# Order of half-width matmuls and of three groups of loads in the gradient tail of a memory transformer

## The chip, the core and the metric

The kernel runs on one core of a Trainium2 chip. The metric is the device time of one execution in microseconds (us), as the median of several runs. The engines named here are TensorE (PE; its weight loads are shown apart as PEld), VectorE (DVE), ScalarE (ACT), GpSimd (POOL) and SyncE (SP). POOL and SP issue most of the transfers (DMAs) of this kernel: SP those of its own queue, plain and transposing, POOL those of another.

## The reference

One transformer layer, forward and backward. Attention runs over segments of 32 rows that carry 8 memory rows from one segment to the next, and a gated feed-forward block follows. All ten results (the output and nine gradients) are returned.

```
x = A_x                                   # 1 x 2048 x 448
h = x + A(layernorm(x), mem0, Wq, Wk, Wv, Wo)     # 64 segments, one after another
h2 = h + (silu(n @ w_gate) * (n @ w_up)) @ w_down  # n = layernorm(h)
outputs: h2 and the gradients of A_x, mem0, Wq, Wk, Wv (448 x 16 x 256 each),
         Wo (16 x 256 x 448), w_gate, w_up (448 x 1792), w_down (1792 x 448)
```

In each segment `A` concatenates the memory (8 rows) and 32 rows of x, projects them to q, k and v for 16 heads of 256, applies a masked softmax, and its first 8 output rows are the memory of the next segment. So the gradients of Wq, Wk, Wv and Wo are products over 2048 token rows and 512 memory rows, which is 20 blocks of 128 rows: 16 token blocks and 4 memory blocks. The gradients of the feed-forward weights are products over the 16 token blocks.

## The kernel before

The kernel has a forward chain over 64 segments, a feed-forward phase, a backward chain over the 64 segments, and a tail (`tail_phase`, from L1289) that computes the weight gradients from operands that the earlier phases have stored in DRAM. The change concerns the tail and the first loads for it.

**Units of the tail.** First comes the gradient of Wo, in two halves of the columns. `rows_by_d` (L1392) takes 6, 5 or 5 column tiles at a time; with every one of the 20 blocks of rows it does one matmul for each tile (L1397), of an X_o tile against a block of DCt, the stored gradient of the output. Then come the halves v0, v1, k0, k1, q0, q1 of the gradients of Wv, Wk and Wq (`att`, L1420), with `up_grad` for w_gate (DGP) after v0 and for w_up (DU) after k0, and at the end w_down, again with `rows_by_d`.

**d_by_e (L1365)** computes 448 rows of a gradient by 1024 columns. The 448 rows are three full tiles of 128 and a rest of 64. For each block there are six full-width matmuls (L1375: three row tiles by two column groups of 512) and two half-width ones (L1380), which put their 64 rows into the two halves of one accumulator. Full-width ones come in groups of four blocks. The half-width ones follow each group where the argument `frees` is true; where it is false they all come at the end of the pass, after the last group. `att` and `up_grad` call `d_by_e` twice for each unit: the first pass (q = 0, or p0 = 0) with `frees` false, the second with `frees` true.

**Memory blocks.** The four memory blocks of a unit are not stored in the layout that the tail needs. `load_m` (L1336) makes three steps for each: `fetch` (L1340), a DMA from POOL into one of two buffers; `pack`, a copy half by VectorE (L1345) and half by ScalarE (L1347); and `turn`, twice eight transposes on PE (L1354) into the one transposing bank, each emptied by a copy (L75 or L76) into a ring slot. In a first pass they are put ahead of the groups of four blocks: the pack of memory block 0 and the fetch of block 2 before block 0; turn 0, pack 1 and fetch 3 before block 4; turn 1 and pack 2 before block 8; turn 2 and pack 3 before block 12; turn 3 before block 16. The transposes are recorded to issue after `k.last_mm`, the last matmul recorded then. The fetches of blocks 0 and 1 are made in the pass before.

**Order.** A scheduler orders each engine's instructions from the recorded program, so that a line of the program and its place in a queue need not be the same. VectorE, ScalarE, POOL and SP take their instructions in that order. On SP each load waits for the landing of the load eight before it, and POOL keeps a like rule.

**Loads for the tail.** `_TailLoads` (L314) hands out ring slots. In the last segment of the backward chain (s == 0) `grads(0)` loads DCt: four loads for the memory blocks (L342), then eight that gather the token blocks row by row (L346 and L347, 24 and 8 partitions each). Then `outs(0, 7, 0, 6)` loads the first six column tiles of X_o for the first seven blocks in the order of use, in which the four memory blocks come first. More calls of `outs` follow. Each load is recorded to issue after `k.last_load`, the last load of the backward chain. The gradient of w_down needs grad_out, which is loaded by POOL (L1471) into the space in which HN, the operand of `up_grad`, has lain.

Of the kernel before, what the change touches and what calls it, by code (L numbers as in the profile page):

```python
# [15 lines left out]
P = 128  # L16
# [297 lines left out]
class _TailLoads:  # L314
# [12 lines left out]
    def ring(self):  # L327
        if self.first:
            return self.first.pop(0)
        self.n += 1  # L330
        return self.slots[(self.n - 1) % len(self.slots)]

    def grads(self, part):
        k, D, S, NT, M, SEG = self.k, self.k.D, self.k.S, self.k.NT, self.k.M, self.k.SEG
        sync, DHb = k.nc.sync, k.dr["DHb"]
        dcx = DHb[0:S, 0:D].rearrange("(t r i) d -> r i t d", r=4, i=SEG)
        dcm = DHb[S:, 0:D].rearrange("(t r m) d -> r m t d", r=4, m=M)
        dc8 = DHb[0:S, 0:D].rearrange("(g s i) d -> g s i d", s=16, i=SEG)
        if part == 0:
            for g in range(k.NB - NT):  # L340
                with k.tc.issue_after(k.last_load.ins):
                    sync.dma_start(out=self.DCt[:, NT + g], in_=dc8[g, :, 0:M])  # L342
        for r in range(4):
            if part == 0:
                with k.tc.issue_after(k.last_load.ins):
                    sync.dma_start(out=self.DCt[32 * r:32 * r + 24, :NT], in_=dcx[r, M:SEG])  # L346
                    sync.dma_start(out=self.DCt[32 * r + 24:32 * r + 32, 4:NT], in_=dcm[r, :, 4:NT])  # L347
            else:
                sync.dma_start(out=self.DCt[32 * r + 24:32 * r + 32, 0:4], in_=dcm[r, :, 0:4])
# [682 lines left out]
def backward_chain(k: _K):  # L1032
    nc, tc = k.nc, k.tc
    S, D, M, H, Dh, HD = k.S, k.D, k.M, k.H, k.Dh, k.HD
    SEG, L, NSEG, NT, KC, DP, MC, DC = k.SEG, k.L, k.NSEG, k.NT, k.KC, k.DP, k.MC, k.DC
# [95 lines left out]
    for s in range(NSEG - 1, -1, -1):  # L1131
# [12 lines left out]
        with k.prio.crit():  # L1144
            pss = [k.ps1() for _ in range(4)]
            for j in range(MC):
                c = cj(j)
                b, jj = divmod(j, 8)
                for kc in range(KC):
                    with tc.issue_after(k.last_dh.ins) if s == NSEG - 1 and j == 0 and kc == 0 else nullcontext():  # L1150
                        nc.tensor.matmul(pss[b][:, jj * L:(jj + 1) * L], lhsT=WoT_sb[:, kc, c * P:(c + 1) * P],  # L1151
                                         rhs=do_roll[:, kc, sl, :], start=(kc == 0), stop=(kc == KC - 1))
# [17 lines left out]
                                         start=(dc == 0), stop=(dc == DC - 1), skip_group_check=True)  # L1170
            if s == 0:
                k.tl.grads(0)
                k.tl.outs(0, 7, 0, 6)
            pD3 = pD[:, 0:8 * L].rearrange("p (h n) -> p h n", n=L)
            prod = k.f32("f2", 8 * L, "prod")[:].rearrange("p (h n) -> p h n", n=L)
            nc.vector.scalar_tensor_tensor(out=prod, in0=pD3, scalar=k.scale, in1=P_sb, op0=ALU.mult, op1=ALU.mult)
# [30 lines left out]
            for h in range(8):  # L1207
                for g in range(2):
                    nc.tensor.matmul(pT[64 * g:64 * g + L, h * L:(h + 1) * L], lhsT=dS_bd[:, h, g, :],
                                     rhs=ident[:, 64 * g:64 * g + L], start=True, stop=True, skip_group_check=True)  # L1210
# [78 lines left out]
def tail_phase(k: _K):  # L1289
    nc, tc = k.nc, k.tc  # L1290
    S, D, M, H, Dh, HD, F = k.S, k.D, k.M, k.H, k.Dh, k.HD, k.F
    SEG, L, NSEG, NT, KC, DP, MC, DC, FC = k.SEG, k.L, k.NSEG, k.NT, k.KC, k.DP, k.MC, k.DC, k.FC
# [6 lines left out]
    NB = k.NB  # L1299
# [4 lines left out]
    HC = A(0, NB, D)  # L1304
# [5 lines left out]
    def resbuf():  # L1310
        ri[0] += 1
        return res_b[ri[0] % len(res_b)]

    def accs(n):
        return [k.ps1() for _ in range(min(n, 5))] + [k.fx1() for _ in range(max(0, n - 5))]
# [3 lines left out]
    def evac(out, in_):  # L1319
        eng = "vs"[k._evac_i % 2]  # L1320
        k._evac_i += 1
        k.last_ev[eng] = k.evac(out, in_, eng)

    def load_x(nm, hf):
        tiles = {}
        for t in (range(NT) if nm != "o" else order):
            x_t = ring()
            src = dr["X_" + nm][t][:, hf * 2048:(hf + 1) * 2048]
            if nm == "o":
                nc.sync.dma_start(out=x_t, in_=src)  # L1330
            else:
                nc.sync.dma_start_transpose(out=x_t.rearrange("p (j n) -> p j n", n=P), in_=src)
            tiles[t] = x_t
        return tiles
# [27 lines left out]
    tl.outs(0, NB, 11, 16)  # L1362
    xo = tl.x

    def d_by_e(lhs_of, rhs_of, nblk, widths, store, at=None, frees=True):  # L1365

        pa = accs(7)
        for b0 in range(0, nblk, 4):
            for fn in (at or {}).get(b0, ()):
                fn()  # L1370
            for b in range(b0, min(nblk, b0 + 4)):
                for kc in range(KC - 1):
                    for g in range(2):
                        w = widths[g]
                        k.last_mm = nc.tensor.matmul(pa[2 * kc + g][:, 0:w], lhsT=lhs_of(b)[:, kc * P:(kc + 1) * P], rhs=rhs_of(b, g),  # L1375
                                         start=(b == 0), stop=(b == nblk - 1), skip_group_check=True)
            for b in range(b0, min(nblk, b0 + 4)) if frees else range(nblk) if b0 + 4 >= nblk else ():
                for g in range(2):
                    w = widths[g]
                    k.last_mm = nc.tensor.matmul(pa[6][64 * g:64 * g + 64, 0:w], lhsT=lhs_of(b)[:, (KC - 1) * P:D], rhs=rhs_of(b, g),  # L1380
                                     start=(b == 0), stop=(b == nblk - 1), skip_group_check=True)
        for i in range(6):
            kc, g = divmod(i, 2)
            res = resbuf()
            evac(res[:, 0:widths[g]], pa[i][:, 0:widths[g]])
            store(kc, g, res[:, 0:widths[g]])
        res = resbuf()
        for g in range(2):
            evac(res[64 * g:64 * g + 64, 0:widths[g]], pa[6][64 * g:64 * g + 64, 0:widths[g]])
            store(KC - 1, g, res[64 * g:64 * g + 64, 0:widths[g]])  # L1390

    def rows_by_d(lhs_of, rhs_of, nblk, n, store):  # L1392
        pa = accs(n)
        m = len(nblk) - 4
        for bi, i in [(bi, i) for bi in range(m) for i in range(n)] + [(bi, i) for i in range(n) for bi in range(m, m + 4)]:
            b = nblk[bi]
            k.last_mm = nc.tensor.matmul(pa[i][:, 0:D], lhsT=lhs_of(b, i), rhs=rhs_of(b), start=(bi == 0), stop=(bi == m + 3))  # L1397
        for i in range(n):
            res = resbuf()
            evac(res[:, 0:D], pa[i][:, 0:D])  # L1400
            store(i, res[:, 0:D])
# [15 lines left out]
    HN = W(0, NB, D)  # L1417
    halves = [(nm, oi, hf) for (nm, oi) in (("v", 5), ("k", 4), ("q", 3)) for hf in range(2)]

    def att(hi, mem, after):  # L1420
        nm, oi, hf = halves[hi]
        o2 = OUT[oi].rearrange("d h e -> d (h e)")
        xt = load_x(nm, hf)
        for g in range(NG):
            xt[NT + g] = ring()
        for q in range(2):
            at = {}
            if q == 0:
                (f0, p0, t0), (f1, p1, t1), (f2, p2, t2), (f3, p3, t3) = mem
                at = {0: [p0, f2], 4: [lambda: t0(xt[NT]), p1, f3], 8: [lambda: t1(xt[NT + 1]), p2],  # L1430
                      12: [lambda: t2(xt[NT + 2]), p3], 16: [lambda: t3(xt[NT + 3])]}
            elif after is not None:
                at = {12: [after[0][0], after[1][0]]}

            def st(kc, g, r, q=q, hf=hf, o2=o2):
                e0 = (16 * g + 8 * hf + 4 * q) * P
                nc.gpsimd.dma_start(out=o2[kc * P:min(D, (kc + 1) * P), e0:e0 + 512], in_=r)  # L1437

            def rhs(b, g, q=q, xt=xt):
                return xt[b].rearrange("p (cl g n) -> p cl g n", g=2, n=P)[:, 4 * q:4 * q + 4, g, :]  # L1440
            d_by_e(lambda b: HC[:, b, :], rhs, NB, (512, 512), st, at, q == 1)

    def up_grad(nm, oi, after):
        xt = []
        for t in range(NT):
            x_t = ring()
            nc.sync.dma_start(out=x_t[:, 0:F], in_=dr[nm][t * P:(t + 1) * P, :])
            xt.append(x_t)
        for p0 in (0, 1024):
            ws = (512, min(512, F - p0 - 512))  # L1450

            def st(kc, g, r, p0=p0, oi=oi):
                f0 = p0 + 512 * g
                nc.gpsimd.dma_start(out=OUT[oi][kc * P:min(D, (kc + 1) * P), f0:f0 + r.shape[-1]], in_=r)

            def rhs(b, g, p0=p0, ws=ws, xt=xt):
                return xt[b][:, p0 + 512 * g:p0 + 512 * g + ws[g]]
            d_by_e(lambda b: HN[:, b, :], rhs, NT, ws, st, {8: [after[0][0], after[1][0]]} if p0 else None, p0 > 0)

    mems = [load_m(nm, hf) for (nm, _, hf) in halves] + [None]  # L1460
    mems[0][0][0]()
# [1 line left out]
    for hi in range(len(halves)):  # L1463
        att(hi, mems[hi], mems[hi + 1] if hi not in (0, 2) else None)
        if hi == 0:
            nc.gpsimd.dma_start(out=HN[:, 0:NT, :], in_=dr["HN"].rearrange("(t p) d -> p t d", p=P))
            up_grad("DGP", 7, mems[1])
        if hi == 2:
            up_grad("DU", 8, mems[3])
            GO = W(0, NB, D)  # L1470
            nc.gpsimd.dma_start(out=GO[:, 0:NT, :], in_=GO2.rearrange("(t p) d -> p t d", p=P))  # L1471

# [5 lines left out]
    for j0 in (0, 7):  # L1478
        def st(i, r, j0=j0):
            (nc.gpsimd if j0 == 0 or i % 2 else nc.sync).dma_start(out=OUT[9][(j0 + i) * P:(j0 + i + 1) * P, :], in_=r)  # L1480
        rows_by_d(lambda b, i, j0=j0: zt[b][:, (j0 + i) * P:(j0 + i + 1) * P], lambda b: GO[:, b, :], range(NT), 7, st)

# [34 lines left out]
```

## Time and profile before

Four runs took 3105.69, 3101.58, 3098.59 and 3091.68 us, median 3100.09. The profiled execution is the one of 3105.69 us; its span from the first to the last instruction is 3103.9 us, with a mean granted TensorE clock of 0.988. Over the whole span PE is busy 94%, DVE 43%, ACT 36% and POOL 22% of the time, and the mean transfer rate is 177 GB/s.

The tail by stages (us from the start of the span):

| stage | from | to | us | PE busy |
|---|---|---|---|---|
| before the first matmul of the tail | 2400.00 | 2412.77 | 12.77 | 0.83 |
| gradient of Wo | 2412.77 | 2537.76 | 124.99 | 123.40 |
| v0 | 2537.76 | 2620.37 | 82.61 | 68.00 |
| w_gate (DGP) | 2620.37 | 2664.72 | 44.35 | 43.98 |
| v1 | 2664.72 | 2736.68 | 71.96 | 67.44 |
| k0 | 2736.68 | 2803.97 | 67.29 | 65.77 |
| w_up (DU) | 2803.97 | 2848.31 | 44.34 | 43.97 |
| k1 | 2848.31 | 2921.57 | 73.26 | 67.20 |
| q0 | 2921.57 | 2988.22 | 66.65 | 65.76 |
| q1 | 2988.22 | 3053.90 | 65.68 | 65.68 |
| w_down and the last stores | 3053.90 | 3103.90 | 50.00 | 42.55 |

Each stage begins with its first matmul. The six attention halves do the same work on PE, so their lengths can be compared directly; what exceeds 65.7 us is waiting, or work at a lower clock. Where PE is busy and granted its full clock, a stage is as long as its matmuls.

### The profile page before, as it was taken

The numbers are of one execution on the slowest core, as the hardware profiler recorded it, in microseconds if no ns is written. First come the engines' busy times: TensorE is split into PE (matmuls) and PEld (weight loads), VectorE is DVE, ScalarE is ACT, GpSimd is POOL, SyncE is SP. The second block draws the span as 40 slices with busy tenths as digits, with TensorE's granted clock in tenths as the row PEclk, the third lists the DMA queues.
The fourth block names the chain that finished last, engine by engine and source line by source line (L and its number), as shares of the span: only waits on it lengthen the run. The fifth ranks groups of instructions, "written<-read, shape, count | busy, mean of one in ns | idle before, by whom it ended". The sixth has DMA issues, their size and how long they took to land.

```text
span 3103.9 us, 108337 instructions
## 1 busy us (share of the span) xinstructions
PE 2904.8 (94%) x47640; PEld 1737.9 (56%) x47650; DVE 1333.6 (43%) x3381; ACT 1115.3 (36%) x2634; POOL 675.0 (22%) x1507
## 2 busy tenths in 40 slices
PE   5999999999998999989999999999999989999999
PEld 3455555555544556666666676666666444444444
DVE  4555555555555577744444444444444001111110
ACT  2444444444444454434344443444443001111110
POOL 2222222222222222412211212121121111212111
PEclk9999999999999999999999999999999999999999
DMA  6567766766767999874554445445555998969951
GB/s 242 136 170 180 182 172 171 192 165 170 198 171 181 283 219 237 219 263 122 154 135 140 132 131 159 136 132 142 133 147 162 295 229 213 178 181 219 185 160 51
DMA packets 739468, 550.12 MB, mean 177 GB/s; under 512 B 600052, under 2 KB 635364, under 8 KB 736564
## 3 DMA queue, kind: packets, MB, share of 16 engines
q1 hardware_dynamic: 687956, 389.65, 51.9%
q0 software_dynamic: 51040, 153.54, 14.9%
q8 instruction: 374, 6.13, 0.8%
q14 instruction: 98, 0.80, 0.1%
HBM read 168.01 MB, written 234.23 MB: 130 GB/s over the span
## 4 chain that ended last, share of the span: by engine, by line
PE 67%; issue 14%; DMA 6%; DVE 6%; ACT 3%; POOL 2%; SPq 1%; POOLq 0%; ACTq 0%; DVEq 0%
PE po L1200 7%; PE psf L1151 7%; PE psf L535 6%; PE psf L652 5%; PE po L697 4%; PE psf L1128 4%; PE psf L890 4%; PE fx L1264 3%; PE psf L1375 3%; PE fx L1014 2%; PE fx L464 2%; PE psf L1222 2%; DVE arA L75 2%; PE psf L549 2%; PE psf L1160 2%
## 5 line engine op out<-in xcount | busy, mean ns | idle before, releaser
L75 DVE CAST arA<-psf 128x256 bf16<-128x256 f32 (+3 forms) x933 | 428.4, 480 | 785.1 <-PE psf L1375 233.6
L76 ACT CAST arA<-psf 128x96 bf16<-128x96 f32 (+5 forms) x915 | 353.6, 409 | 1014.7 <-PE psf L1375 254.7
L1200 PE MATMUL po<-arW,arA 128*32 128x448 bf16 x6144 | 348.1, 356 | 4.3 <-DMA arW<-Tq 3.9
L1375 PE MATMUL psf<-arW,arA 128*128 128x512 bf16 x980 | 250.6, 383 | 0.0
L1375 PEld LDWEIGHTS <-arA 128*128 128x128 bf16 x1440 | 137.3, 99 | 168.1 <-issue 19.6
L1151 PEld LDWEIGHTS <-arW 128*128 128x128 bf16 x8192 | 214.0, 96 | 23.5 <-issue 23.5
L1151 PE MATMUL psf<-arA,arW 128*128 128x40 bf16 x8192 | 217.5, 180 | 5.1 <-DVE arA L1226 5.1
L1200 PEld LDWEIGHTS <-arA 128*32 128x32 bf16 x6144 | 152.0, 96 | 116.1 <-ACT arA L76 9.5
L652 PE MATMUL psf<-arW,arA 128*64 128x512 bf16 x1536 | 216.5, 382 | 0.0
L535 PE MATMUL psf<-arW,arA 128*32 128x512 bf16 x3072 | 193.8, 385 | 12.5 <-DVE arA L738 12.5
L76 ACT CAST arB<-psf 128x64 bf16<-128x64 f32 (+3 forms) x384 | 121.9, 318 | 151.5 <-PE psf L539 108.1
L890 PE MATMUL psf<-arW 128*128 128x256 bf16 (+1 forms) x1288 | 148.0, 275 | 3.4 <-DVE arA L75 2.1
L697 PE MATMUL po<-arW,arA 128*32 128x256 bf16 (+1 forms) x4096 | 141.1, 263 | 10.7 <-DVE arA L75 7.7
L890 PEld LDWEIGHTS <-arW 128*128 128x128 bf16 (+1 forms) x1344 | 103.0, 97 | 54.7 <-issue 43.0
L1397 PE MATMUL psf<-arW 128*128 128x448 bf16 x525 | 112.6, 356 | 13.2 <-DMA arW<-X_o 13.2
L1161 ACT COPY arA<-psf 128x1024 bf16<-128x1024 bf16 x128 | 123.3, 1015 | 2.3 <-PE psf L1160 0.8
L1128 PEld LDWEIGHTS <-arW 128*128 128x128 bf16 x2048 | 86.7, 99 | 62.6 <-issue 58.0
L535 PEld LDWEIGHTS <-arA 128*32 128x32 bf16 x3072 | 70.5, 96 | 90.1 <-DVE arA L738 18.1
L76 ACT COPY arA<-psf 128x512 bf16<-128x512 bf16 (+3 forms) x142 | 84.4, 595 | 89.1 <-DVE arA L75 77.3
L464 PE MATMUL fx<-arA,arW 128*128 128x64 bf16 (+1 forms) x2048 | 84.6, 195 | 32.0 <-ACT arB L76 19.0
L1437 POOL DMA_DIRECT2D out_dram<-arA x96 | 52.0, 548 | 275.7 <-DVE arA L75 275.2
L697 PEld LDWEIGHTS <-arA 128*32 128x32 bf16 x4096 | 93.6, 96 | 32.7 <-DVE arA L75 10.9
(286 smaller groups left out, 4626.0 us busy)
## 6 DMA issues: line engine op xcount, KB each, us to landing
arW<-T SPq DMA_DIRECT2D x256, 128.0 KB
X_o<-arA SPq DMA_DIRECT2D x37, 512.0 KB
T<-arA SPq DMA_DIRECT2D x64, 256.0 KB
X_v<-arA POOLq DMA_DIRECT2D x32, 512.0 KB, 4.9
X_k<-arA POOLq DMA_DIRECT2D x32, 512.0 KB, 3.9
X_q<-arA POOLq DMA_DIRECT2D x32, 512.0 KB, 3.1
out_dram<-arA POOLq DMA_DIRECT2D x90, 128.0 KB, 3.8
VG<-arA SPq DMA_DIRECT2D x64, 160.0 KB
```

Source lines behind the costliest of these rows:

```text
L75: return nc.vector.tensor_copy(out=out, in_=in_)
L76: return nc.scalar.copy(out=out, in_=in_)
L464: nc.tensor.matmul(banks[w][:, i * 64:(i + 1) * 64], lhsT=lhsT, rhs=xr[lo:hi, kc, :], start=(kc == 0 and i == 0), stop=(kc == KC - 1), ski ...
L535: nc.tensor.matmul(banks[w][32 * q:32 * q + 32, :], lhsT=hT_roll[:, kc, sl, M:L], rhs=(Wq_sb, Wk_sb)[w][:, kc, col(q, b)], start=(kc == 0) ...
L652: nc.tensor.matmul(pV[b][64 * g:64 * g + 64, 0:512], lhsT=hT_flat[:, kc, sl * L:sl * L + 64], rhs=Wv_sb[:, kc, n * 512:(n + 1) * 512], sta ...
L697: nc.tensor.matmul(pO[32 * q:32 * q + 32, 0:w], lhsT=xblk[:, j, r * SEG:(r + 1) * SEG], rhs=Wo_sb[:, cj(j), 256 * dh:256 * dh + w], start= ...
L890: nc.tensor.matmul(ps[fp][:, f2 * 256:(f2 + 1) * 256], lhsT=Wt[lo:hi, kc, c * P:(c + 1) * P], rhs=xT[lo:hi, kc, :], start=(kc == 0 and f2 ...
L1128: nc.tensor.matmul(ps[b][:, i * 2 * L:(i + 1) * 2 * L], lhsT=lhs[:, at, :], rhs=rhs_bd[:, cl // 2, :, :].rearrange("p g n -> p (g n)"), st ...
L1151: nc.tensor.matmul(pss[b][:, jj * L:(jj + 1) * L], lhsT=WoT_sb[:, kc, c * P:(c + 1) * P], rhs=do_roll[:, kc, sl, :], start=(kc == 0), stop ...
L1161: nc.scalar.copy(out=dO_sb[:, 8 * hf:8 * hf + 8, :], in_=ph.rearrange("p (c n) -> p c n", n=P))
L1200: nc.tensor.matmul(pH[32 * (j % 4):32 * (j % 4) + 32, 0:D], lhsT=blk[nm][:, j, r * SEG:(r + 1) * SEG], rhs=WT[:, cj(j), :], start=(nm == " ...
L1375: k.last_mm = nc.tensor.matmul(pa[2 * kc + g][:, 0:w], lhsT=lhs_of(b)[:, kc * P:(kc + 1) * P], rhs=rhs_of(b, g), start=(b == 0), stop=(b = ...
```

## The change

There are three parts. First, the argument `frees` is gone: in every pass the half-width matmuls follow each group of four blocks, and `k.last_mm` is set by the half-width matmuls alone. Second, grad_out is loaded at `hi == 3`, after the unit k1 in the program, and not at `hi == 2`, after the w_up unit. Third, `grads(0)` itself loads X_o for the four memory blocks, between its loads for the memory blocks of DCt and the eight for the token blocks, and the call of `outs` that follows starts at the fifth block. `outs` itself is unchanged. No operand, size or result changes.

```diff
@@ grads @@
             for g in range(k.NB - NT):
                 with k.tc.issue_after(k.last_load.ins):
                     sync.dma_start(out=self.DCt[:, NT + g], in_=dc8[g, :, 0:M])
+            self.outs(0, k.NB - NT, 0, 6)
         for r in range(4):
             if part == 0:
                 with k.tc.issue_after(k.last_load.ins):
@@ backward_chain @@
             if s == 0:
                 k.tl.grads(0)
-                k.tl.outs(0, 7, 0, 6)
+                k.tl.outs(4, 7, 0, 6)
@@ tail_phase @@
-    def d_by_e(lhs_of, rhs_of, nblk, widths, store, at=None, frees=True):
+    def d_by_e(lhs_of, rhs_of, nblk, widths, store, at=None):
...
                     for g in range(2):
                         w = widths[g]
-                        k.last_mm = nc.tensor.matmul(pa[2 * kc + g][:, 0:w], lhsT=lhs_of(b)[:, kc * P:(kc + 1) * P], rhs=rhs_of(b, g),
+                        nc.tensor.matmul(pa[2 * kc + g][:, 0:w], lhsT=lhs_of(b)[:, kc * P:(kc + 1) * P], rhs=rhs_of(b, g),
                                          start=(b == 0), stop=(b == nblk - 1), skip_group_check=True)
-            for b in range(b0, min(nblk, b0 + 4)) if frees else range(nblk) if b0 + 4 >= nblk else ():
+            for b in range(b0, min(nblk, b0 + 4)):
                 for g in range(2):
                     w = widths[g]
                     k.last_mm = nc.tensor.matmul(pa[6][64 * g:64 * g + 64, 0:w], lhsT=lhs_of(b)[:, (KC - 1) * P:D], rhs=rhs_of(b, g),
...
-            d_by_e(lambda b: HC[:, b, :], rhs, NB, (512, 512), st, at, q == 1)
+            d_by_e(lambda b: HC[:, b, :], rhs, NB, (512, 512), st, at)
...
-            d_by_e(lambda b: HN[:, b, :], rhs, NT, ws, st, {8: [after[0][0], after[1][0]]} if p0 else None, p0 > 0)
+            d_by_e(lambda b: HN[:, b, :], rhs, NT, ws, st, {8: [after[0][0], after[1][0]]} if p0 else None)
...
         if hi == 2:
             up_grad("DU", 8, mems[3])
+        if hi == 3:
             GO = W(0, NB, D)
             nc.gpsimd.dma_start(out=GO[:, 0:NT, :], in_=GO2.rearrange("(t p) d -> p t d", p=P))
```

## The prediction

> **What bounds the kernel now.** I read four views of the kernel before: the stretches by stage (the table above), what TensorE waited for in the tail, the timeline around those waits, and the DMA issues inside them. The two changed functions run only at the very end of the backward pass and in the tail, so only the last 720 us matter. In that tail TensorE is busy 654.6 of 703.9 us; its idle time is a handful of waits:
>
> ```profile
> PE ph L1354 <- DVE arW L75: 27.6, 5, 14.6
> PE psf L1397 <- DMA arW<-X_o: 13.2, 3, 11.6
> ```
>
> Columns: who waits, for whom, us in total, times, longest. The five waits of L1354 all stand at one place, the second half of the second memory block (the transposes due before block 8) of a first pass (q = 0): 14.62 us in v0, 4.52 in v1, 1.52 in k0, 6.06 in k1, 0.89 in q0, none in q1. The timeline of k1 shows what ends such a wait:
>
> ```profile
> 2851.84 1.19 POOL L1471 DMA_DIRECT2D arW<-in_grad_out_dram  x1
> 2853.02 0.78 POOL L1340 DMA_DIRECT2D arA<-M_k  x1
> ...
> 2866.11 0.43 DVE L1345 COPY arA<-arA 128x1024 bf16<-128x1024 bf16 x1 [11.27 <-DMA arA<-M_k]
> 2866.45 0.68 DVE L75 COPY arW<-ph 128x1024 bf16<-128x1024 bf16 x1
> ...
> 2867.19 1.01 PE L1354 MATMUL ph<-ident,arB 128*128 128x128 bf16 x8 [6.06 <-DVE arW L75]
> 2867.99 0.63 PE L1375 MATMUL psf<-arA 128*128 128x512 bf16 x1
> ```
>
> Columns: start, duration, engine, line, what, count, idle time before it. Read from below: PE waits for VectorE's copy out of the one transpose bank; VectorE, in order, stands at the pack of memory block 2; that pack waits for the M_k fetch. The fetch was issued at 2853.02 behind the load of grad_out and landed 13.0 us later by the DMA view, which gives grad_out 1,792 KB and 12.6 us. So the wait ends 1.17 us after a DMA landing (2867.19 less 2866.02), not after any PE work.
>
> How the half-width matmuls (L1380) cost today, in the first pass and in the second:
>
> ```profile
> 2584.27 0.38 PE L1375 MATMUL fx<-arW,arA 128*128 128x512 bf16 x1
> 2584.58 0.62 PE L1380 MATMUL fx<-arA 128*64 128x512 bf16 x4
> 2585.03 4.05 PE L1380 MATMUL fx<-arW,arA 128*64 128x512 bf16 x36
> 2589.02 1.25 PE L1375 MATMUL psf<-arA 128*128 128x512 bf16 x5
> ...
> 2593.99 0.38 PE L1375 MATMUL fx<-arW,arA 128*128 128x512 bf16 x1
> 2594.30 0.62 PE L1380 MATMUL fx<-arA 128*64 128x512 bf16 x4
> 2594.76 0.60 PE L1380 MATMUL fx<-arW,arA 128*64 128x512 bf16 x4
> 2595.29 1.25 PE L1375 MATMUL psf<-arW,arA 128*128 128x512 bf16 x5
> ```
>
> From the last full-width start before to the first one after them, less one full-width step of 0.216 (1.08 us for five in the same timeline): one block of 40 costs 4.75 - 0.22 = 4.53, a block of 8 costs 1.30 - 0.22 = 1.08. In up_grad the first pass has one block of 32, 2640.88 to 2644.77: 3.89 - 0.22 = 3.67.
>
> The start of the tail, on SP and PE:
>
> ```profile
> 2384.18 3.02 SPq L342 DMA_DIRECT2D arW<-DHb  x4
> 2387.25 0.78 SPq L346 DMA_DIRECT2D arW<-DHb  x1
> ...
> 2398.56 1.97 SPq L347 DMA_DIRECT2D arW<-DHb  x1
> 2400.57 3.17 SPq L356 DMA_DIRECT2D arW<-X_o  x3
> 2404.44 8.88 SPq L356 DMA_DIRECT2D arA<-X_o  x6
> ...
> 2412.77 2.05 PE L1397 MATMUL psf<-arW 128*128 128x448 bf16 x5 [11.61 <-DMA arW<-X_o]
> ```
>
> PE stands 11.61 us until the first X_o is there. By stretches, the DMA share is 0.98, 1.06, 0.91, 0.94, 1.06 and 1.08 in the six 4-us slices from 2388 to 2412: the transfers, not the issue, are full.
>
> **What the skill says.** TensorE: Matmul & The Clock Gate, Part 1: the clock halves after an idle window of about 3.4 us and returns after a busy one, windows free-running. The trace agrees: after the 4.52 us wait the 20 full-width matmuls of block 8 on took from 2682.55 to 2688.28 and not 4.1; after the 1.52 us wait nothing slowed. TensorEngine Tiling, Key Properties: a change of tiling mode drains the array. The trace has it as the difference of 5 x 1.08 and 4.53. DMA: Bandwidth & Descriptors, Issuing engines are not separate DMA queues: all queues share 16 engines; the full shares above agree. Same page, Why a DMA increments its semaphore by 16 (how many engines): a load whose outer dimension is 24 or 8 uses 12 or 8 engines only. No run here shows the engine of a packet, but L346 and L347 (24 and 8 rows) are those loads, and they are the slow ones here.
>
> **Part 1, half-width matmuls in groups.** In the program built from the change, every first pass has on PE: 24 full-width, 8 half-width, 8 transposes, 4 full-width, 8 transposes, 20 full-width and so on; the orders of VectorE and ScalarE are unchanged. Cost: six units of 20 blocks, 5 x 1.08 - 4.53 = 0.89 each, 5.3; two of 16, 4 x 1.08 - 3.67 = 0.65 each, 1.3; +6.6 us. Gain: before the waiting transposes PE now does two half-width blocks, 2.17 us, that used to follow the wait. The wait ends with a landing whose fetch is issued at the start of the unit, so these 2.17 us disappear in it: 2.17 + 2.17 + 1.52 + 0.89 = 6.75 in v0, v1, k0, q0. The wait left in v1 is 2.35 us; whether the clock still drops is open: one cold window of 3.41 us costs 1.7, so 0 to 1.7, I take 0.9 saved. In v0 the wait stays at 12.4, clock as before. The accumulators are freed later at the end of a first pass (8 half-width matmuls behind them, not 40); the second pass ends so today, and the next unit starts 0.31 us after, so nothing. Sum of part 1: 6.6 - 6.75 - 0.9 = -1.0.
>
> **Part 2, grad_out a unit later.** On POOL the load only moves behind the two M_k fetches of the same unit, ahead of the M_q ones. Those two then go right behind the eight stores L1454, landed by 2856.2. Other units without such a load in front: fetch to landing 11.7, 9.7, 7.4 and 7.5 us. From 2851.84 that is 2859.2 to 2863.5, and with 1.17 the transposes may run at 2860.4 to 2864.7. PE, with its two half-width blocks, gets there at about 2863.1 (2860.97 + 2.17). So the 6.06 us go, and with them the cold time (2867.19 to 2870.15 at half speed, 1.5): -7.5 at best, and -3 if 1.6 of wait and a cold window of up to 1.7 remain. I take -7.5, since three of the four fetches are fast enough. Where grad_out goes instead, 2856 to 2870, nobody waits for it before 3053.9, and the M_q fetches behind it are needed at 2921.6.
>
> **Part 3, memory blocks first.** Four X_o loads of 192 KB move ahead of eight DHb loads on SP. PE gets them around 2398 (the DHb loads in that place landed from 2394 to 2400) and does 24 matmuls of 0.19 = 4.5 us that stood at 2412.77 to 2417.85. But blocks 5 to 20 need all eight DHb loads and their own X_o; the bytes ahead of block 5's X_o are the same, and that stretch is full. Block 5 then starts between 2414.5 and 2417, on a cold clock (up to 2.5 us lost, while the 1.5 lost today lie in blocks 1 and 2). Bounds: -3.3 to +1. Later in the stage PE waits again for X_o, 0.63 and 0.96 us at 2494 to 2496, and that stream is full throughout, so part of any gain is returned there. I take -0.7.
>
> **Sum.** -1.0 - 7.5 - 0.7 = -9.2: span 3103.9 to 3094.7. The profiled run took 3105.69, at the upper end of the four; against their median, 3100.09, the same 9.2 us give 3091. About 0.3%, 9.3 us, is what a measurement of this kernel can tell from no change.
>
> **The rivals.**
> - The M_k fetch is slow by itself. In v1 nothing stands ahead of it and it took 11.7 us beside the X_k transposes. Then a wait of about 2 us and a cold window stay, part 2 gives 3.8, the sum is -5.5: 3094.6. For: k1 runs beside the X_q transposes. Against: q0 and q1, 7.4 and 7.5.
> - More than forecast: no cold window in v1 (-0.8 more), part 3 at its bound (-2.6 more), v0 back to full clock sooner (-0.8): -13.4, 3087. For: all three depend on where the windows of the clock fall. Against: the full DMA.
> - Slower: the wait does not shrink when PE comes later, because the landing comes later as well. The two half-width blocks then push the transposes back, and grad_out, now beside block 2's and 3's fetches, holds k1 as long as before. All 6.6 us of part 1 stay, part 3 adds 1: +7.6, 3107.7. It decides as soon as landings move by over 2.2 us a unit. Against: fetches are issued after the packs of block 0, which PE doesn't delay.
>
> **How the numbers follow.** Forecast 0.50, slow fetch 0.25, more 0.19, slower 0.06. The forecast lies at the 0.3% bound, so half of it (0.25), most of the larger gain (0.18) and some of the slow-fetch case by scatter (0.08) are faster: 0.51; slower by over 0.3% is what scatter adds to the last rival, and something unseen: 0.06; the rest, 0.43, within. The scatter of the four runs, 8 down to 6 up around the median, is as large as the effect. Range: from -13.4 to -5.5, some 7 more below and 5 above for scatter: 3080 to 3100.
>
> **What would show it.** In the changed profile: the second half of the memory transposes before block 8 waits about 12.4, 2.3, 0, 0, 0, 0 us in the six units; the stretch of k1 shrinks from 73.3 to about 66.6 and q1, which has no wait, grows from 65.7 to about 66.6; up_grad from 44.35 to about 45.0; the first L1397 start comes near 2399 instead of 2412.8, with a new wait before block 5. It would be wrong if k1 keeps over 2 us of wait, or if waits before block 8 keep their length.

## The result, and the profile after

Before: 3099.21 us, the median of 64 runs (3083.94 to 3124.04). After: 3090.85 us, of 43 runs (3081.04 to 3108.08). The ratio is 0.9973, 95% interval 0.9961 to 0.9984: some 8.4 us, or 0.27%, less. 9.2 us were forecast.

What TensorE (PE) waits for in the tail of the changed kernel (who, for whom, us in total, times, longest):

```profile
PE psf L1398 <- DMA out_dram<-arB: 12.6, 1, 12.6
PE ph L1355 <- DVE arW L75: 4.0, 1, 4.0
PE psf L1398 <- DMA arW<-X_o: 0.8, 1, 0.8
```

Line numbers of the tail are one higher than before (that of the load of grad_out two). Of the five waits of the memory transposes (27.6 us) one is left, 4.0 us in v0; 12.4 in v0 and 2.3 in v1 were forecast. The stretches of v0, w_gate, v1, k0, w_up, k1, q0 and q1 in the same profile, in this order; columns: from and to, length, then busy time of PE, of its weight loads, DVE, ACT and POOL, the granted clock, the DMA share and GB/s:

```profile
2549.20:2622.52 73.32, 69.30 (x386) 30.82 (x384) 8.72 (x16) 12.17 (x16) 10.62 (x18) 0.95 0.84 237
2622.52:2667.55 45.03, 44.66 (x254) 21.49 (x257) 4.84 (x8) 3.75 (x8) 8.53 (x17) 1.00 1.06 196
2667.55:2734.13 66.58, 66.58 (x385) 29.90 (x385) 9.64 (x17) 12.11 (x16) 11.73 (x21) 1.00 0.94 211
2734.13:2800.72 66.59, 66.59 (x387) 29.91 (x385) 9.40 (x16) 12.32 (x16) 11.73 (x21) 1.00 0.65 165
2800.72:2845.75 45.03, 44.66 (x254) 21.47 (x257) 4.83 (x8) 3.75 (x8) 8.52 (x17) 1.00 0.99 194
2845.75:2912.33 66.58, 66.58 (x385) 29.89 (x385) 9.64 (x17) 12.11 (x16) 12.89 (x22) 1.00 1.10 216
2912.33:2978.92 66.59, 66.59 (x387) 29.88 (x385) 9.50 (x16) 12.42 (x16) 11.72 (x21) 1.00 0.94 208
2978.92:3045.51 66.59, 66.59 (x387) 29.90 (x385) 9.40 (x16) 12.31 (x16) 10.22 (x19) 1.00 0.27 93
```

From v1 on the length of every attention half is its PE busy time: it is bound by its matmuls alone. q1, which had no wait before, went from 65.68 to 66.59; the up_grad units from 44.35 to 45.03. This is the price of the grouping, as forecast (66.6 and 45.0).

k1 in the timeline (start, duration, engine, line, what, count, idle time before it and what ended it):

```profile
2849.27 0.78 POOL L1341 DMA_DIRECT2D arA<-M_k  x1
2850.22 0.77 POOL L1341 DMA_DIRECT2D arB<-M_k  x1 [0.17 <-issue]
...
2852.06 1.16 POOL L1473 DMA_DIRECT2D arW<-in_grad_out_dram  x1 [1.08 <-DMA out_dram<-arA]
...
2855.26 0.43 DVE L1346 COPY arA<-arA 128x1024 bf16<-128x1024 bf16 x1 [1.90 <-DMA arA<-M_k]
...
2860.66 0.61 PE L1355 MATMUL ph<-ident,arB 128*128 128x128 bf16 x8
```

grad_out now follows the two M_k fetches. The pack of block 2 starts 6.0 us after its fetch, and the transposes, 5.4 us later, wait for nothing. Before, 13.1 us lay between fetch and pack.

The start of the tail:

```profile
2396.16 2.89 SPq L342 DMA_DIRECT2D arW<-DHb  x4
...
2399.10 2.38 SPq L357 DMA_DIRECT2D arW<-X_o  x3
...
2401.59 0.88 SPq L357 DMA_DIRECT2D arA<-X_o  x1
2402.51 0.46 SPq L347 DMA_DIRECT2D arW<-DHb  x1
...
2410.40 0.93 PE L1398 MATMUL psf<-arW 128*128 128x448 bf16 x4
...
2429.27 2.05 PE L1398 MATMUL psf<-arW,arA 128*128 128x448 bf16 x5 [12.59 <-DMA out_dram<-arB]
```

The first matmul comes 14.2 us after the first load (28.6 before), and a wait of 12.59 us stands before the fifth block instead of 11.61 before the first. The view names a store (`out_dram<-arB`) as what ended it; in the six other profiles with these loads in front it names the X_o load for the same wait, and this matmul needs that load and all eight of DHb, so it is read here as a wait for loads. v0 starts 153.0 us after the first load; before, 153.6.

The two profiled spans, 3103.9 and 3095.5 us, also differ by 8.4, but that is chance. From the first load (L342) to the end it is 719.7 us before and 699.3 after, 20.4 less: v0 -9.3, k1 -6.7, v1 -5.4, k0 -0.7, the gradient of Wo -0.5, q0 -0.1, against q1 +0.9 and twice +0.7 for up_grad. And the tail starts 12.0 us later. Most of that is one wait in the feed-forward phase, which the change does not touch. What PE waits for from 1200 to 1260 us, after:

```profile
PE fx L1015 <- DVE arW L991: 11.7, 1, 11.7
```

In the profile of before the same line waits 0.3 us. In the twelve profiles of this study the tail starts between 2379.1 and 2396.2 us: the phases ahead of it scatter by 17 us. So two profiles can't be compared by their spans here, only stage by stage; and the first question is how far a single stage scatters from profile to profile.

### The profile page after: what moved, and what is told of

Same layout as the page of the kernel before. It is cut to its first block, busy times and chain, and to the rows that moved or that the text cites. A ratio compares the mean times of both kernels' runs of the same rounds, so it can differ in the third digit from the quotient of the medians.

```text
span 3095.5 us, 108342 instructions
## 1 busy us (share of the span) xinstructions
PE 2908.8 (94%) x47640; PEld 1733.3 (56%) x47650; DVE 1333.7 (43%) x3381; ACT 1115.1 (36%) x2634; POOL 674.0 (22%) x1507
## 3 DMA queue, kind: packets, MB, share of 16 engines
q0 software_dynamic: 51040, 153.54, 15.1%
## 4 chain that ended last, share of the span: by engine, by line
PE 79%; DVE 6%; issue 5%; DMA 4%; ACT 3%; POOL 1%; SPq 1%; ACTq 0%; POOLq 0%; DVEq 0%
PE psf L1376 10%; PE po L1201 7%; PE psf L1152 7%; PE psf L536 6%; PE psf L653 5%; PE po L698 4%; PE psf L1129 4%; PE psf L891 4%; PE fx L1265 3%; PE fx L1015 2%; PE fx L465 2%; PE fx L1381 2%; PE psf L1223 2%; DVE arA L75 2%; PE psf L550 2%
## 5 line engine op out<-in xcount | busy, mean ns | idle before, releaser
L536 PE MATMUL psf<-arW,arA 128*32 128x512 bf16 x3072 | 192.5, 383 | 12.5 <-DVE arA L739 12.5
L1129 PE MATMUL psf<-arB,arW 128*128 128x80 bf16 x2048 | 97.1, 201 | 14.0 <-DVE arB L1182 6.0
```

The source lines that it names most:

```text
L536: nc.tensor.matmul(banks[w][32 * q:32 * q + 32, :], lhsT=hT_roll[:, kc, sl, M:L], rhs=(Wq_sb, Wk_sb)[w][:, kc, col(q, b)], start=(kc == 0) ...
L1129: nc.tensor.matmul(ps[b][:, i * 2 * L:(i + 1) * 2 * L], lhsT=lhs[:, at, :], rhs=rhs_bd[:, cl // 2, :, :].rearrange("p g n -> p (g n)"), st ...
```

## The experiments

The medians are compared with runs of the kernel before on the same chip. "Tail" is from the first load L342 to the end, in the profiled run. The marks tell which of the three parts a kernel has: 1 half-width matmuls in groups, 2 grad_out later, 3 memory blocks first.

| kernel | parts | median us | ratio to before (95%) | tail | v0 | v1 | k0 | k1 |
|---|---|---|---|---|---|---|---|---|
| before | - | 3099.21 | | 719.7 | 82.6 | 72.0 | 67.3 | 73.3 |
| e_group | 1 | 3100.73 | 0.9995 (0.9974 to 1.0016) | 717.8 | 73.0 | 66.6 | 66.6 | 83.9 |
| e_go | 2 | 3092.66 | 0.9980 (0.9963 to 0.9997) | 700.2 | 73.9 | 67.3 | 66.9 | 67.6 |
| e_mem | 3 | 3102.07 | 1.0002 (0.9979 to 1.0025) | 715.1 | 73.5 | 70.7 | 67.7 | 80.5 |
| e_no_group | 2, 3 | 3090.15 | 0.9969 (0.9950 to 0.9987) | 698.8 | 74.6 | 68.1 | 66.5 | 66.3 |
| e_no_go | 1, 3 | 3098.81 | 0.9998 (0.9981 to 1.0016) | 715.7 | 72.1 | 67.8 | 66.6 | 82.8 |
| e_no_mem | 1, 2 | 3086.77 | 0.9966 (0.9949 to 0.9983) | 713.7 | 82.2 | 66.6 | 66.6 | 72.0 |
| after | 1, 2, 3 | 3090.85 | 0.9973 (0.9961 to 0.9984) | 699.3 | 73.3 | 66.6 | 66.6 | 66.6 |
| e_hn | 1, 2, 3, HN later | 3084.76 | 0.9956 (0.9939 to 0.9972) | 700.0 | 66.6 | 66.6 | 66.6 | 72.9 |
| e_early | 1, 2, 3, early fetches | 3079.48 | 0.9931 (0.9907 to 0.9954) | 693.4 | 66.6 | 66.6 | 66.6 | 66.6 |
| e_best | 2, 3, early fetches | 3073.07 | 0.9905 (0.9882 to 0.9929) | 686.6 | 65.7 | 65.7 | 65.7 | 65.7 |
| e_early_only | early fetches | 3080.07 | 0.9932 (0.9907 to 0.9958) | 686.7 | 65.7 | 65.7 | 65.7 | 65.7 |

**One part alone.** e_group is the kernel before with only the diff of `d_by_e` and its calls.

> Only the half-width matmuls in groups of four blocks; grad_out and the first X_o loads as before. Theory (the prediction's part 1): the median moves by -1.0 us (+6.6 for more switches, -7.6 taken from the waits); waits before block 8 of about 12.4 us in v0, 2.3 in v1, 3.9 in k1 and 0 in k0, q0, q1, and w_gate and w_up at 45.0 us each. Rival 1 (landings move with TensorE): the waits stay at 14.6, 4.5, 1.5, 6.1, 0.9 and the median rises by 6 us or more. Rival 2 (part 1 alone made v0 short): v0 waits about 4 us, as in the changed kernel, and the median falls by 8 or more. Rival 3 (the landing of the fetch in v0 differs from run to run by as much as 8 us, whatever the parts): the v0 wait is anywhere from 4 to 13 us.

What PE waits for in its tail:

```profile
PE ph L1354 <- DVE arW L75: 21.1, 3, 15.1
PE psf L1397 <- DMA arW<-X_o: 12.2, 2, 11.8
```

The median did not move (0.9995, -1.6 us, with 6.5 us either side). That agrees with the theory and speaks against rival 1; the fall of 8 us or more of rival 2 lies at the edge of the interval. The wait in v0 is the short one that rival 2 names, but the next two kernels, without this part, have a short one too. The waits are not the forecast ones either: 4.6 us in v0 and 15.1 in k1, where 12.4 and 3.9 were expected. k1 got worse by 9 us with grad_out where it was before. Rival 3, the scatter of landings, is right about the single waits.

e_go is the kernel before with only this:

```diff
+        if hi == 3:
             GO = W(0, NB, D)
```

> Only the load of grad_out behind the two M_k fetches of k1; half-width matmuls and first loads as before. Theory (the prediction's part 2): the wait in k1 before block 8 goes from 6.06 us to 0 to 2 us (PE is 2.17 us earlier there than in the changed kernel), k1 from 73.3 to 66 to 68.5 us, the median by -5.5 to -7.5 us; v0, v1, k0 wait as before (14.6, 4.5, 1.5 us). Rival (the M_k fetch is slow by itself): a wait of 3 us or more and a cold clock stay, the median moves by no more than -3.8. Rival 3 (scatter of the landings): the waits of the units that the edit does not touch differ from before by several us as well.

```profile
PE psf L1397 <- DMA arW<-X_o: 12.8, 2, 11.8
PE ph L1354 <- DVE arW L75: 12.2, 5, 6.7
```

k1 fell to 67.6 us and the median by 6 (ratio) to 8 (medians), as the theory said. But v0, which this edit does not touch, waited 6.7 us and not 14.6: rival 3 again, the scatter of the landings.

e_mem is the kernel before with only the two edits of `outs`.

> Only the X_o loads of the four memory blocks ahead of the eight DHb loads of the token blocks. Theory (the prediction's part 3): the first matmul of the gradient of Wo comes about 14 us after the first DHb load instead of 28.6, a new wait of about 12 us stands before its fifth block, and the first matmul of v0 comes 153 us after the first DHb load as before (153.6), within -3.3 and +1; the median moves by less than 2 us. Rival (the early blocks are a gain of their own): v0 starts 4 us or more earlier and the median falls by 4. A second rival, that the shorter wait in v0 of the changed kernel (4.0 for 14.6 us) came from this part: then it is near 6 us here, and 14.6 if not.

```profile
PE ph L1355 <- DVE arW L75: 24.4, 4, 13.3
PE psf L1398 <- DMA arA<-X_o: 12.5, 1, 12.5
```

The first matmul came 14.5 us after the first load, the fifth block waited 12.5 us, v0 started after 152.8 us, and the median stayed. The wait in v0 was 6.0 us, which the second rival claims for this part; but e_group and e_go, without it, had short ones as well.

**One part left out.** e_no_group, e_no_go and e_no_mem are the changed kernel with one of these diffs reversed.

> The changed kernel without part 1: half-width matmuls of a first pass at its end again, the other two parts kept. Theory (part 1 is a trade of 2.17 us less in each wait for 0.89 us in each of six units and 0.68 in each of two): the units without a wait take 65.7 us and not 66.6, w_gate and w_up 44.35 and not 45.03, and the wait in v0 is about 6.2 us (4.0 to 4.6 with groups, 6.0 and 6.7 without); the median is within 3 us of the changed kernel's 3091. Rival (part 1 carries the gain): 3097 or more. For the fetches: one that SP's last transposing load precedes by 2 us or more lands in 5 to 7 us and leaves no wait or one below 2 us, one that it precedes by less than 1.3 us lands in 9 to 15 us and leaves 2 us or more.

> The changed kernel without part 2: grad_out ahead of the M_k fetches of k1 again, the other two parts kept. Theory (the load in front of the fetches is worth more than the one profile of before showed): the wait in k1 is 4 to 15 us (6.1, 15.1 and 13.3 in the three profiles with grad_out in front), k1 takes 71 to 84 us, and the median is 7 to 10 us above the changed kernel's 3091. Rival (as forecast, about 7.5, of which the two half-width blocks hide 2.2): k1 takes no more than 71 us and the median is 5 us above or less.

> The changed kernel without part 3: the X_o loads of the four memory blocks after the eight DHb loads again, the other two parts kept. Theory (the early blocks only move the wait from the first block to the fifth): first matmul of the gradient of Wo 29 us after the first DHb load, v0 153 to 154 us after it, median within 2.5 us of the changed kernel's 3091. Rival (part 3 is worth its bound of 3.3 or more): v0 3 us later and a median of 3094 or more.

Without part 1: 3090.15, the same as with it; q0 and q1 at 65.7, up_grad at 44.35, the wait in v0 6.5 us. The rival (3097) falls. Without part 2 nearly all of the gain is gone (3098.81), and k1 takes 82.8 us. Its timeline:

```profile
2856.82 0.43 DVE L1346 COPY arA<-arA 128x1024 bf16<-128x1024 bf16 x1 [20.33 <-DMA arA<-M_k]
2857.16 0.68 DVE L75 COPY arW<-ph 128x1024 bf16<-128x1024 bf16 x1
2857.90 1.01 PE L1355 MATMUL ph<-ident,arB 128*128 128x128 bf16 x8 [14.04 <-DVE arW L75]
```

The chain is the one that the prediction read in k1 of before (fetch, pack, copy, transposes), with 14.04 us at its end instead of 6.06: the M_k fetch behind grad_out landed after 23.2 us. Without part 3: 3086.77, 4 us below the changed kernel where 2.5 were allowed (2 us by the ratios, 0.9966 and 0.9973, whose intervals overlap), but away from the rival's 3094; v0 starts 153.1 us after the first load. This profile has the other long wait of v0:

```profile
PE ph L1354 <- DVE arW L75: 16.7, 2, 12.7
```

Of the 16.7 us, 12.7 are in v0 and 4.0 in k1. So v0 has two cases. With HN in front of the M_v fetches (eight profiles, all but e_hn and the three with early fetches) the fetch landed after 14.8 to 15.8 us in six and after 23.6 and 23.8 in two, the kernel before and e_no_mem; in these HN itself took 21.9 and 22.2 us, not 13.2 to 14.1. What makes it one or the other stayed open: both are without part 3, but so are e_group and e_go, which had the short case.

**Size of each part.** With all eight combinations run, each part's effect is the mean of four differences of ratios, with and without it, times 3100 us: part 1 -1.5, part 2 -8.3, part 3 +0.1 us, each with some 4 us either side (the root of the summed squares of the intervals' half-widths, over four). So the medians tell part 2 alone from nothing. In the profiles k1 takes 80.1 us on average in the four kernels with grad_out in front and 68.1 in the four with it behind, 12.0 us less and not 8.3. One profile of each kernel can't say which is nearer.

**The wait that is left.** e_hn does with HN in v0 what part 2 does with grad_out in k1:

```diff
-                nc.gpsimd.dma_start(out=ld, in_=dr["M_" + nm][g * 4:(g + 1) * 4].rearrange(
+                k.last_fetch = nc.gpsimd.dma_start(out=ld, in_=dr["M_" + nm][g * 4:(g + 1) * 4].rearrange(
...
-            nc.gpsimd.dma_start(out=HN[:, 0:NT, :], in_=dr["HN"].rearrange("(t p) d -> p t d", p=P))
+            with tc.issue_after(k.last_fetch.ins):
+                nc.gpsimd.dma_start(out=HN[:, 0:NT, :], in_=dr["HN"].rearrange("(t p) d -> p t d", p=P))
```

> The changed kernel with the load of HN, the operand of w_gate, issued after the two M_v fetches of v0 and not before them, as part 2 does with grad_out. Theory (the fetch that ends the wait in v0 lands late because the 1,792 KB of HN stand ahead of it): the wait in v0 goes to 0 to 2 us, v0 takes 66.6 to 69 us, and the median is 4 to 10 us below the changed kernel's 3091, so 3081 to 3087; w_gate starts without a wait, since HN is issued about 65 us before it. Rival (the transposing loads of X_v and the loads of DGP fill the 16 engines, and the fetch is late anyway): a wait of 3 us or more stays in v0 and the median is within 2 us of 3091.

```profile
PE psf L1398 <- DMA arA<-X_o: 13.4, 1, 13.4
PE ph L1355 <- DVE arW L75: 4.6, 1, 4.6
```

v0 has no wait and takes 66.58 us, the median is 3084.76: the theory holds. It is the stretch that shows it; the ratios of e_hn and of the changed kernel, 0.9956 and 0.9973, have overlapping intervals. The 4.6 us are in k1, where the changed kernel had none, although nothing of k1 was edited and grad_out stands behind the fetches in both. SP's and POOL's issues around the first M_k fetch, first in e_hn:

```profile
2834.88 0.54 POOL L1455 DMA_DIRECT2D out_dram<-arA  x1
...
2835.03 4.01 SPq L1333 DMA_TRANSPOSE arW<-X_q  x1
2835.41 0.78 POOL L1341 DMA_DIRECT2D arA<-M_k  x1
```

and in the changed kernel:

```profile
2845.73 3.53 SPq L1333 DMA_TRANSPOSE arW<-X_q  x1
...
2847.62 1.60 POOL L1455 DMA_DIRECT2D out_dram<-arA  x3
...
2849.27 0.78 POOL L1341 DMA_DIRECT2D arA<-M_k  x1
```

In e_hn the fetch follows a transposing load of SP by 0.38 us and landed after 14.9 us; in the changed kernel by 3.54 us, and landed after 5.9. It is so in all fetches of block 2 that have no large load in front, in v0, v1, k1 and q0 of the first nine kernels of the table: nine issued at most 0.41 us after such a load landed after 7.9 to 14.9 us, fifteen issued 1.6 us or more after one landed after 5.2 to 7.9. (In k0 and q1 no transposing load had been issued for some 20 us or more, and the fetch took 7.1 to 10.1 us beside plain loads.) The expectation of e_no_group had said so beforehand, and its v1 (0.41 us, landed after 9.6, a wait of 2.3) and k1 (3.78 us, after 5.6, no wait of 1 us) bore it out. It is a sorting of what happened; no run moved the one load against the other on purpose, and it does not carry over to other fetches. In q0 five fetches for the next half (its first block), issued 1.5 to 1.7 us after a transposing load, landed after 10.5 to 18.3 us, and one issued 0.03 us after such a load (e_no_mem) after 5.5. So what makes a fetch slow stays open.

**Fetches a stage earlier.** If every wait before block 8 is the landing of a fetch issued at the start of its own unit, the place to mend is the issue. In e_early the packs of blocks 0 and 1 and the fetches of 2 and 3 go to the last group of the stage before:

```diff
-                at = {0: [p0, f2], 4: [lambda: t0(xt[NT]), p1, f3], 8: [lambda: t1(xt[NT + 1]), p2],
+                at = {4: [lambda: t0(xt[NT])], 8: [lambda: t1(xt[NT + 1]), p2],
...
-                at = {12: [after[0][0], after[1][0]]}
+                at = {12: [after[0][0], after[1][0]], 16: [after[0][1], after[2][0], after[1][1], after[3][0]]}
```

with the same at block 12 of `up_grad`, and for v0 before the last five tiles of the gradient of Wo. e_best is this with part 1 undone, e_early_only this with none of the three parts.

> The changed kernel, in which the packs of memory blocks 0 and 1 and the fetches of blocks 2 and 3 come a stage earlier: in the last group of the stage before (for v0, before the last five tiles of the gradient of Wo), so that no fetch of a unit waits behind HN, grad_out or the transposing loads at its own start. Theory (every wait before block 8 is the landing of a fetch that is issued at the start of the unit): no wait in any unit, six times 66.6 us, v0 6 to 7 us shorter than in the changed kernel, median 3081 to 3085. Rival (VectorE or ScalarE now stands at a pack and empties the accumulators or the transposing bank late): new waits of TensorE at the ends of second passes, 1 us or more each, and a median of 3089 or more.

> The same earlier packs and fetches, with the half-width matmuls of a first pass at its end again, as in the kernel before (part 1 undone). Theory (part 1 only pays while there is a wait to fill): six units of 65.7 us and two of 44.35, 0.9 x 6 + 0.7 x 2 = 6.7 us less than with groups, median 3075 to 3079. Rival (a fetch or a pack is still late, and the transposes before block 8 wait again, since TensorE is 2.2 us earlier there): a wait in two or more units and a median of 3082 or more.

> The kernel before with the earlier packs and fetches alone, none of the three parts. Theory (all three parts treat, or pay for, waits that this takes away at the root; grad_out then stands behind the fetches of k1 by itself): no wait in any unit, six times 65.7 us, median 3072 to 3076, the same as with parts 2 and 3 (3073). Rival (part 2 or part 3 is still worth something beside it): 3078 or more, with a wait in k1 or a v0 that starts 3 us later after the first DHb load.

e_early has no wait of the transposes in any unit, and with 3079.48 us it is 1.5 below the range expected; e_best is 1.9 below its own. In e_best v0, w_gate and v1 are the first three stretches:

```profile
2535.11:2600.78 65.67, 65.67 (x385) 30.54 (x384) 7.95 (x14) 10.18 (x14) 9.13 (x16) 1.00 0.98 260
2600.78:2645.13 44.35, 44.35 (x258) 22.00 (x257) 5.16 (x10) 5.74 (x10) 10.14 (x19) 1.00 1.06 218
2645.13:2710.81 65.68, 65.68 (x385) 30.53 (x385) 9.80 (x18) 12.00 (x16) 11.81 (x21) 1.00 0.91 215
```

Each is its PE busy time at full clock, beside a DMA share of 0.91 to 1.06; and so are the other five. The median, 3073.07 (0.9905, 0.9882 to 0.9929), is below both kernels. e_early_only has no wait either and the same tail, 686.7 for 686.6 us; its wait at the start is before the first block again, and v0 starts after 153.9 us against 153.8. Its median, 3080.07, missed the 3072 to 3076 expected and lies where the rival put it (3078 or more), but neither sign that the rival named is there, no wait in k1 and no later start of v0. In the profiled runs its tail starts 10 us later than that of e_best, in code that is the same. With six runs of each (3071.33 to 3084.04; 3069.67 to 3077.20) the medians can't settle whether parts 2 and 3 are worth something beside the early fetches. The tails show nothing that they would be worth.

## Why the prediction was right, and where it was not

- **Its sum**, -9.2 us, was measured as -8.4. The interval, -12.1 to -5.0 us, also holds the -5.5 of the first rival, so it is the stages that decide between them, and not the total. The parts came out as -1.5 (forecast -1.0), -8.3 (-7.5) and +0.1 (-0.7), each within its error of 4 us.
- **Part 1.** The costs were right to 0.03 us: +0.91 us in q1 (0.89), +0.68 for each up_grad unit (0.65). The gain of 2.17 us is borne out between like cases of v0: 14.6 us without groups and 12.7 with them among the long waits, 6.0 to 6.7 without and 3.7 to 4.6 with them among the short ones. What failed is the wait itself: "In v0 the wait stays at 12.4" took the 14.62 of one profile for the length of that wait, and that was the case of two profiles in eight. That the changed kernel's profile shows 4.0 is the change's doing by some 2 us only. The same for "The wait left in v1 is 2.35 us": the fetch landed after 9.2 us instead of 11.7.
- **Part 2.** The mechanism was right. The term of 7.5 us was mis-sized twice, in opposite directions. With grad_out in front the M_k fetch landed after 20.3, 23.2 and 24.0 us in the three other profiles and k1 took 80.5 to 83.9; the 13.0 us and 73.3 of before were the best of four. And with grad_out behind, the wait does not always go: "since three of the four fetches are fast enough" missed that 4.0 and 4.6 us remain in e_no_mem and e_hn, where the fetch was issued 0.27 and 0.38 us after a transposing load. That was the rival of the slow fetch, right in two of the five kernels with part 2 and without early fetches. One sum is wrong as well: 7.5 less 1.6 of wait and 1.7 of cold window leaves 4.2, and not 3; nothing else was built on it.
- **Part 3.** As forecast in place: first matmul early, a new wait before block 5, nothing left of the 14 us. The start of v0 after the first load is 153.1 to 153.6 us in four profiles without it and 152.8 to 153.3 in four with it (154.1 in e_hn). Block 5 began 33.1 us after the first load; the 2414.5 to 2417 of the prediction are 30.3 to 32.8, so it came a little after that range. One reading was off: the DHb loads of before that stand in the place of the four X_o loads had not all landed by 2400; the semaphore updates of the profile put the landing of the third at 2403.4. That the bytes ahead of block 5 set this is the prediction's argument; no run took bytes away.
- **The rivals.** "Slower" asked for landings that move with PE by over 2.2 us. In like cases they do not: in the short v0 cases the M_v fetch landed 17.7 to 18.3 us after the start of v0 without groups and 17.5 to 18.5 with them.

So the total was right partly by luck, because two errors in reading one profile lie on opposite sides: v0 of before was 8 to 9 us longer than in the three short cases without groups, k1 7 to 11 us shorter than in the three others with grad_out in front. A forecast that kept v0's long wait and removed k1's short one came out near the mean.

## What to carry to other kernels

A wait that ends with a transfer has a distribution, not a length: before a single profile's wait goes into a sum, see how the same stage fares in profiles of other kernels that leave it alone, or give it a range. Where an operand is fetched at the start of the stage that needs it, move the fetch into the stage before; that removed all the waits before block 8 here, while filling them with other work paid some 2 us for each wait and cost 0.7 to 0.9 us in every unit, waiting or not. And ask of each moved load what stands in front of it, on its own queue and on the other ones.

## What was not expected of the hardware

The Trainium skill says (DMA: Bandwidth & Descriptors, Issuing engines are not separate DMA queues) that transfers of all engines run on the same 16 engines and interleave. The runs agree and show how uneven that is for one load: the same 512 KB fetch of block 2 took 5.2 to 14.9 us with nothing large in front, 7.9 us or more in the nine cases in which a transposing load of another queue had been issued at most 0.41 us before it, and 13.0 to 24.0 us with 1,792 KB in front of it on its own queue. And runs of the same code ahead of the tail differ by up to 17 us, more than any part of the change moved the median.
